# Seven block products for eight: the output product of a gated linear unit as 2x2 blocks, in a kernel whose instruction order is planned

## The chip, the cores and the metric

One core of one Trainium2 chip. The metric is the device time of one execution in microseconds (us), median of several; the profile adds the span of one profiled execution, which is some 2 us shorter. Engines are named as in the profile: PE = TensorE (matmul), PEld = TensorE's weight load (runs beside PE), DVE = VectorE, ACT = ScalarE, POOL = GpSimd, SP = SyncE (here: issues transfers). PSUM is the memory on the chip that this kernel's matmuls write to, in *banks*; SBUF holds the rest.

## The reference, cut to what matters

```python
# q, k, v: (8 batches, 8 heads, 576, 64); w_val, w_out: (512, 512); conv_w: (5, 512); all fp32
kv  = einsum('bhsd,bhse->bhde', k, v)
x   = einsum('bhsd,bhde->bhse', q, kv)
x   = x / sqrt(mean(x*x, -1) + 1e-6) * g_norm        # then heads are put side by side: (8, 576, 512)
gate_pre[:, s] = sum over j in 0..4 of conv_w[j] * x[:, s - 4 + j]   # causal, per channel
out = (sigmoid(gate_pre) * (x @ w_val)) @ w_out
```

The last product, `gv @ w_out` with `gv = gate * val`, is the *output product*. The change is about it.

## The kernel before, in the parts that matter

Tokens of two batches are cut into nine chunks of 128; the middle one belongs to both batches. For each chunk, four matmuls of 512 columns sum over 512 channels into a PSUM bank, ScalarE copies the bank to SBUF, and SyncE stores it:

```python
def out_product(i, c):
    po = ps("mm", [P, C], f"out{i}_{c}")                 # "mm": a ring of three PSUM banks
    for jt in range(NK):                                 # NK = 4, C = 512, P = 128
        nc.tensor.matmul(po[:], gv[:, jt, c * P:(c + 1) * P], wout[:, jt, :],
                         start=(jt == 0), stop=(jt == NK - 1))
    st["po", i, c] = po

def keep_out(i, c):
    ot = work.tile([P, C], FP32, tag="ot", bufs=3, name=f"ot{i}_{c}")
    nc.scalar.copy(out=ot[:], in_=st["po", i, c][:])
    st["ot", i, c] = ot
```

What VectorE does ahead of it, per batch and group of 128 channels (four such groups): four *taps* of the convolution on 576 tokens, each reading what the one before wrote, and two *gatings* that read the value product from a PSUM bank of the same ring of three:

```python
def gate_tap(b, jt, tap):
    gate = st["gate", b, jt]
    nc.vector.scalar_tensor_tensor(
        out=gate[:], in0=xTs[b % 3][:, jt, tap * TB:tap * TB + S],
        scalar=cwT[:, tap, jt:jt + 1], in1=gate[:], op0=ALU.mult, op1=ALU.add)

def gated(b, jt, n):
    first = b % 2 * S + n * SV
    nc.vector.tensor_tensor(
        out=gv[:, jt, first:first + SV], in0=st["val", b, jt, n][:],
        in1=st["gate", b, jt][:, n * SV:(n + 1) * SV], op=ALU.mult)
```

Nothing of this is issued in the order of the text. Every step is given to a planner with its engine, an assumed duration, a wished time, and what it needs, takes and frees; the planner finds one order for all engines, and the instructions are issued in it. Each engine then works through its own queue strictly in order. A table of shifts, found by search, moves the wished times:

```python
SHIFTS = {"gate_start": {0: 7}, "gate_tap": {3: 16.5, 7: 9}, ...}      # cut: 22 kinds of steps

def add(self, engine, time, want, fn, *args, needs=(), gives=(), takes=(), frees=(), ...):
    ...
    want += SHIFTS.get(fn.__name__, {}).get(which[0] if len(which) == 1 else which, 0.0)
    ...
...
    for step in plan.order():
        step["fn"](*step["args"])
```

Of the kernel before, what the change touches and what calls it, by code (L numbers as in the profile page):

```python
# [15 lines left out]
P = 128  # L16
# [5 lines left out]
    "gate_start": {0: 7},  # L22
    "gate_tap": {3: 16.5, 7: 9},
    "gated": {0: 14.5, 6: -13.5},
    "halo": {2: -0.5, 4: -69, 6: -5.5},
    "kv_product": {1: -16, 6: -3},
    "load_half": {("k", 3): -7, ("k", 4): -27, ("k", 6): -21.5, ("v", 0): -5, ("v", 1): 18, ("v", 2): -5,
        ("v", 4): -34, ("v", 6): -74},
    "load_q": {3: 2.5, 4: -1, 5: -3, 6: -5, 7: -12.5},
    "load_q_rows": {0: -273, 1: 28.5},  # L30
    "load_tails": {0: -53, 3: -20.5, 4: 24},
    "move_blocks": {3: 35, 7: 5.5},
    "narrow_weight": {("wout", 1): -14.5, ("wout", 2): -68},
    "normalise": {2: -16.5},
    "out_product": {2: -291.5},
    "powers": {7: -166.5},
    "raw_product": {0: -10.5},
    "square": {1: 0.5, 5: -17.5},
    "stage_weight": {("cw", 0): -385, ("wout", 0): -43, ("wout", 3): -18.5, ("wval", 1): -83.5,
        ("wval", 2): -40, ("wval", 3): -31.5},  # L40
    "store": {0: -1.5},
    "sums": {0: -19, 2: -73.5, 4: 6},
    "turn_q": {3: -15, 5: -59.5},
    "turn_x": {0: -9.5},
    "val_product": {0: 15, 1: 47.5, 2: 72, 3: 70.5, 4: 57, 5: 52},
# [3 lines left out]
class Planner:  # L49
# [7 lines left out]
    HOP = 0.15  # L57
    LANDING = 1.9

    def __init__(self, rings, by_batch):  # L60
        self.by_batch = by_batch
        self.rings = {name: {"size": n, "taken": [], "freed": {}} for name, n in rings.items()}
        self.steps, self.done, self.pending = [], {}, []

    def add(self, engine, time, want, fn, *args, needs=(), gives=(), takes=(), frees=(), load=0.0, ahead=40.0):
# [5 lines left out]
            gives=list(gives), takes=list(takes), frees=list(frees), load=load, ahead=ahead, at=len(self.steps)))  # L71

    def ready(self, step):

        t = step["want"] - step["ahead"]
        for key in step["needs"]:
            if key not in self.done:
                return None
            when, engine = self.done[key]
            t = max(t, when + (0.0 if engine == step["engine"] else self.HOP))  # L80
        for name, owner in step["takes"]:
            ring = self.rings[name]
            n = len(ring["taken"]) - ring["size"]
            if name in self.by_batch and len(ring["taken"]) != owner:
                return None
            if n >= 0:
# [4 lines left out]
                t = max(t, when + (0.0 if engine == step["engine"] else self.HOP))  # L91
        return t

    def order(self):
        free, transfers, left, found = {}, 0.0, list(self.steps), []
        while left:
# [20 lines left out]
            for name, owner in step["frees"]:  # L117
                self.rings[name]["freed"][owner] = end, step["engine"]
# [6 lines left out]
def kernel(  # L125
# [10 lines left out]
):  # L136

# [47 lines left out]
    def ps(kind, shape, name):  # L185
# [3 lines left out]
        "k0": 2, "k1": 2, "v0": 2, "v1": 2, "tails": 2, "q": 4, "w64": 3, "y": 2, "wexp": 2, "wman": 1,  # L189
# [20 lines left out]
    wout = const.tile([P, NK, C], FP32, name="wout")  # L210

# [77 lines left out]
    def narrow(key, dst, n):  # L289
# [40 lines left out]
        else:  # L330
            nc.vector.scalar_tensor_tensor(
                out=dst, in0=split(mf), scalar=gcol[:] if key[0] == "wval" else 2.0 ** -20, in1=split(e.bitcast(FP32)),
# [53 lines left out]
    def turn_q(b, hp):  # L386

        q, qT = st["q", b, hp], new_qT(b)[:, hp, :]
        for c in range(NJ):
            nc.vector.transpose(out=qT[:, c * P:(c + 1) * P], in_=q[:, c:NJ * HB:NJ, 0:TB])  # L390
# [109 lines left out]
    def turn_blocks(b, c):  # L500
        if ("y", b) not in st:
            st["y", b] = work.tile([P, C // TB, NJ, TB], FP32, tag="y", name=f"y{b}")
# [66 lines left out]

    def store(i, c):  # L570
# [13 lines left out]
    def before(kind, n, b):  # L584
        return [(kind, b, ORDER[n - 1])] if n else []

    def attention(b, first, step, kv_first, turn_first):

        slow = 1.7 if b == 0 else 1.0
        for hp in range(HP):  # L590
# [9 lines left out]
            if b >= TURNED:  # L600
                plan.add(
                    "DVE", 1.0, turn_first + 1.5 * hp, turn_q, b, hp,
# [4 lines left out]
            "ACT", 0.8, kv_first + 1.5 * HP, kv_copy, b,  # L607
# [3 lines left out]
        if b < TURNED:  # L611
            parts = [("qT", b, j) for j in range(NJ + 1)]
            for n, j in enumerate(ORDER):
# [9 lines left out]
                    "ACT", 0.95, turn_first + 0.8 * n + 0.8, sort_q, b, j,  # L623
# [5 lines left out]
        for n, c in enumerate(ORDER):  # L629
# [11 lines left out]
                "ACT", 0.62 * part, t + 1.0, square, b, c, needs=[("raw", b, c)], gives=[("sq", key)],  # L641
# [3 lines left out]
                "DVE", 0.7 * part, t + 1.6, sums, b, c, needs=[("sq", key)], gives=[("ss", key)],  # L645
# [7 lines left out]
                "DVE", 0.7 * part, t + 4.2, normalise, b, c, needs=[("raw", b, c), ("rt", key)],  # L653
                gives=[("x", key)], takes=[("x", key)], frees=[(bank, ("raw", key)), ("rt", key)],
            )
            if b >= TURNED and c < NJ:
                plan.add(
                    "DVE", 0.75, t + 5.5, turn_blocks, b, c,
# [9 lines left out]
                "ACT", 0.72 * part, t + 6.2, keep_x, b, c, needs=[("px", key)] + before("xT", n, b),  # L668
# [19 lines left out]
    def gates(b, first, step):  # L688
        for jt in range(NK):
            t = first + jt * step  # L690
            key = b, jt
            plan.add(
                "ACT", 0.8, t, gate_start, b, jt,
# [3 lines left out]
            for n, tap in enumerate(TAPS):  # L697
                plan.add(
                    "DVE", 0.82, t + (n + 1) * step / K, gate_tap, b, jt, tap,
# [3 lines left out]
                "ACT", 0.7, t + step, gate_end, b, jt, needs=[("gate", key, 0)],  # L703
# [3 lines left out]
    DV, DO = 2.5, 4.45  # L707
    HALVES = (range(NJ // 2 + 1), range(NJ // 2, NJ + 1))

    def products(b, first, step):  # L710
        made = []
        for jt in range(NK):
            for n in range(NV - 1, -1, -1):
# [4 lines left out]
                    needs=[("xT", b, c) for c in HALVES[n]] + [("wval", jt)],  # L718
                    gives=[("val", key)], takes=[("mm", ("val", key))],
# [3 lines left out]
                    "DVE", 0.46, t + 2.0, gated, b, jt, n,  # L723
                    needs=[("val", key), ("gate", (b, jt))] + [("gv", k) for k in made], gives=[("gv", key)],
                    takes=[("gv", b)] if jt == 0 and not last else [],
# [4 lines left out]

    def outputs(b, first):

        chunks = range(NJ + 1) if b % 2 == 0 else range(NJ + 1, 2 * NJ + 1)
        for n, c in enumerate(chunks):
            t = first + n * DO
            key = b // 2, c
            used = [b, b + 1] if c == NJ else [b]
# [126 lines left out]
```

## Time and profile before

| | before |
|---|---|
| time, median of 4 runs | 352.77 us (352.19 to 353.3) |
| profiled span | 350.3 us |
| TensorE busy | 327.5 us (93%) |
| VectorE busy | 235.6 us (67%) |
| batch 0 fully gated / batch 1's first gating | 69.9 / 77.8 us |

The two times in the last row are landmarks: the starts of the last instruction `gv<-val,gate` of batch 0, and of the first of batch 1, in VectorE's timeline. The page's second part cuts the span into 40 slices; each digit is the busy share in tenths (PEclk: the granted TensorE clock in tenths). Of the kernel before:

```profile
PE   3576998999999999999999999999999999999994
DVE  3366999899885779459957557997656088980000
PEclk9968999999999999999999999999999999999999
```

TensorE has holes only in the first seven slices, some 60 us, and at the very end. VectorE has air in most slices after the tenth. The prediction below shows the remaining lines of the kernel before.

### The profile page before, as it was taken

What the parts mean: (1) busy time and instruction counts of PE and PEld (TensorE: products, weight loads), DVE (VectorE), ACT (ScalarE), POOL (GpSimd) and SP (SyncE); (2) the same over time, 40 slices, a digit from 0 to 9 for tenths busy, and PEclk for the clock granted to TensorE, in tenths of its full rate; (3) what the DMA queues carried; (4) which work ended last, traced back from release to release, by engine and by line L of the source; (5) the groups of instructions that cost most, each with busy time, mean ns of one, the idle gap of its engine ahead of it and who ended that gap; (6) DMA issues with size and microseconds to landing.
All of it is one profiled execution on the core that took longest, in us unless ns stands there. A gap on an engine that the chain in (4) does not pass through costs nothing.

```text
span 350.3 us, 5671 instructions
## 1 busy us (share of the span) xinstructions
PE 327.5 (93%) x1969; PEld 221.6 (63%) x1969; DVE 235.6 (67%) x484; ACT 124.5 (36%) x229; POOL 128.0 (37%) x178
## 2 busy tenths in 40 slices
PE   3576998999999999999999999999999999999994
PEld 2565877887566557754787457745886467774441
DVE  3366999899885779459957557997656088980000
ACT  3745887173412251243321254333112154211211
POOL 3007215433219845420169960012669930000000
PEclk9968999999999999999999999999999999999999
DMA  6999999992244978973781769923012740002232
GB/s 208 314 304 336 315 242 275 256 278 77 61 129 125 226 251 210 288 169 93 220 224 30 192 154 239 269 71 82 10 31 50 188 125 1 2 0 52 67 89 61
DMA packets 46010, 55.32 MB, mean 158 GB/s; under 512 B 15754, under 2 KB 36254, under 8 KB 45982
## 3 DMA queue, kind: packets, MB, share of 16 engines
q1 hardware_dynamic: 42750, 48.67, 50.7%
q0 software_dynamic: 3072, 6.30, 7.7%
q8 instruction: 15, 0.25, 0.3%
q14 instruction: 13, 0.11, 0.1%
q10 hardware_dynamic: 160, 0.00, 0.0%
HBM read 39.21 MB, written 9.44 MB: 139 GB/s over the span
## 4 chain that ended last, share of the span: by engine, by line
PE 78%; DVE 8%; DMA 7%; ACT 3%; POOL 2%; issue 1%; SPq 1%; DVEq 0%; ACTq 0%; POOLq 0%
PE val L540 33%; PE out L559 30%; PE raw L442 7%; DVE gate L528 4%; PE kv L369 4%; DMA w_wval<-in_moe_w_val_dram 2%; DMA xT<-y 2%; DMA q<-in_q_dram 2%; POOL rt L470 1%; PE xTps L488 1%; PE qTps L403 1%; DVE qT L390 1%; DVE ss L464 1%; DVE x L477 1%; ACT gate L522 0%
## 5 line engine op out<-in xcount | busy, mean ns | idle before, releaser
L540 PE MATMUL val<-xT,wval 128*128 128x288 f32 x512 | 129.7, 408 | 0.0
L559 PE MATMUL out<-wout,gv 128*128 128x512 f32 x288 | 125.4, 592 | 0.0
L528 DVE SCALAR_TENSOR_TENSOR gate<-xT,cwT,gate 128x576 f32<-128x576 f32 x128 | 102.7, 815 | 25.1 <-ACT gate L522 22.9
L470 POOL TENSOR_TENSOR rt<-ss,mhalf 128x8 f32<-128x8 f32 (+1 forms) x40 | 63.8, 1604 | 134.7 <-DVE ss L464 134.4
L540 PEld LDWEIGHTS val<-xT,wval 128*128 128x128 f32 x512 | 95.4, 190 | 26.8 <-issue 1.7
L559 PEld LDWEIGHTS out<-wout,gv 128*128 128x128 f32 x288 | 54.1, 190 | 63.9 <-issue 61.9
L511 POOL DMA_DIRECT2D xT<-y x96 | 52.8, 556 | 17.0 <-DVE y L503 10.7
L567 ACT COPY ot<-out 128x512 f32<-128x512 f32 x36 | 20.9, 584 | 75.9 <-DMA out_dram<-ot 40.4
L442 PE MATMUL raw<-kvbd,qT 128*128 128x128 f32 (+1 forms) x320 | 38.9, 279 | 3.3 <-DVE x L477 2.4
L442 PEld LDWEIGHTS raw<-kvbd,qT 128*128 128x128 f32 (+1 forms) x320 | 35.2, 180 | 10.0 <-issue 3.9
L456 ACT ACTIVATE sq<-raw 128x512 f32<-128x512 f32 (+1 forms) x40 | 22.1, 552 | 53.2 <-PE raw L442 53.1
L535 ACT ACTIVATE gate<-gate 128x576 f32<-128x576 f32 x32 | 21.9, 684 | 48.7 <-DVE gate L528 48.6
L549 DVE TENSOR_TENSOR gv<-val,gate 128x288 f32<-128x288 f32 x64 | 28.3, 453 | 16.0 <-PE val L540 14.6
L464 DVE TENSOR_REDUCE ss<-sq 128x8 f32<-128x520 f32 (+1 forms) x40 | 25.3, 634 | 17.4 <-ACT sq L456 17.4
L477 DVE TENSOR_TENSOR x<-raw,rt 128x512 f32<-128x512 f32 (+1 forms) x40 | 25.2, 629 | 5.9 <-POOL rt L470 5.1
L369 PE MATMUL kv<-v,k 128*64 128x64 f32 x512 | 22.3, 238 | 5.6 <-DMA k<-in_k_dram 5.6
L522 ACT ACTIVATE gate<-xT,cwT 128x576 f32<-128x576 f32 x32 | 23.0, 768 | 11.5 <-DVE gv L549 7.1
L369 PEld LDWEIGHTS kv<-v,k 128*64 128x64 f32 x512 | 19.8, 151 | 9.6 <-issue 8.6
L390 DVE STREAM_TRANSPOSE qT<-q 128x128 f32<-128x128 f32 x96 | 20.7, 274 | 0.2 <-DMA q<-in_q_dram 0.2
L403 PE MATMUL qTps<-ident,q 128*64 128x128 f32 (+1 forms) x160 | 12.2, 317 | 5.5 <-DMA q<-in_q_dram 5.5
L503 DVE STREAM_TRANSPOSE y<-x 128x512 f32<-128x512 f32 x24 | 16.9, 706 | 0.6
L403 PEld LDWEIGHTS qTps<-ident,q 128*64 128x64 f32 (+1 forms) x160 | 10.8, 171 | 6.9 <-POOL vl L218 4.3
(56 smaller groups left out, 119.5 us busy)
## 6 DMA issues: line engine op xcount, KB each, us to landing
q<-in_q_dram SPq DMA_DIRECT2D x96, 140.0 KB, 4.1
out_dram<-ot SPq DMA_DIRECT2D x144, 64.0 KB, 1.7
v<-in_v_dram SPq DMA_DIRECT2D x16, 512.0 KB, 7.7
k<-in_k_dram SPq DMA_DIRECT2D x16, 512.0 KB, 7.2
xT<-y POOLq DMA_DIRECT2D x96, 64.0 KB, 2.8
q<-in_q_dram SPq DMA_DIRECT2D x4, 512.0 KB, 5.6
w_wval<-in_moe_w_val_dram SPq DMA_DIRECT2D x4, 512.0 KB, 8.5
w_wout<-in_moe_w_out_dram SPq DMA_DIRECT2D x4, 512.0 KB, 9.3
```

What stands on the lines that cost most here:

```text
L369: nc.tensor.matmul(kvp[r * D:(r + 1) * D, hp, :], st["k", b, half][:, h, j, :] if j < NJ else kl[:, 2 * hp + r, :], st["v", b, half][:, h, ...
L390: nc.vector.transpose(out=qT[:, c * P:(c + 1) * P], in_=q[:, c:NJ * HB:NJ, 0:TB])
L403: nc.tensor.matmul(pq[r * D:(r + 1) * D, hp, 0:m], st["q", b, half][:, h, j, :] if j < NJ else st["q", b, 2][:, 2 * hp + r, :], ident[0:m, ...
L442: nc.tensor.matmul(raw[row * m:(row + 1) * m, col * P:(col + 1) * P], st["qT", b][:, hp, c * P:c * P + m], kv_bd[b % 2][:, hp, :], start=T ...
L464: nc.vector.reduce_sum(out=ss[:, 0:n], in_=st["sq", b, c][:, 0:n], axis=AX.X)
L470: nc.gpsimd.tensor_tensor(out=rt[:, 0:n], in0=st["ss", b, c][:, 0:n], in1=mhalf[:, 0:n], op=ALU.pow)
L477: nc.vector.tensor_tensor(out=x[:, 0:n * D].rearrange("p (h e) -> p h e", h=n), in0=st["raw", b, c][:, 0:n * D].rearrange("p (h e) -> p h ...
L511: nc.gpsimd.dma_start(out=xTs[b % 3][i * TB:(i + 1) * TB, :, first:first + P], in_=y[a * TB:(a + 1) * TB, i])
L528: nc.vector.scalar_tensor_tensor(out=gate[:], in0=xTs[b % 3][:, jt, tap * TB:tap * TB + S], scalar=cwT[:, tap, jt:jt + 1], in1=gate[:], op ...
L540: nc.tensor.matmul(val[:], wval[:, kc, jt * P:(jt + 1) * P], xTs[b % 3][:, kc, HALO + n * SV:HALO + (n + 1) * SV], start=(kc == 0), stop=( ...
L549: nc.vector.tensor_tensor(out=gv[:, jt, first:first + SV], in0=st["val", b, jt, n][:], in1=st["gate", b, jt][:, n * SV:(n + 1) * SV], op=A ...
L559: nc.tensor.matmul(po[:], gv[:, jt, c * P:(c + 1) * P], wout[:, jt, :], start=(jt == 0), stop=(jt == NK - 1),)
```

## The change

Intent: two chunks of tokens (rows) by the two halves of the channels (columns of `gv`), times `w_out` in 2x2 blocks, is a 2x2 block product. Strassen's scheme, in Winograd's form, does it with seven block products instead of eight, at the price of sums on the inputs and outputs. Sixteen pairs of chunks are done so; the four middle chunks stay as they were.

- Input sums on VectorE: four `token_sums` for two pairs (512 elements each, 32 in all), and four `weight_sums` once.
- Each block product is two matmuls of 256 columns. Partial results a and c share one PSUM bank, b has its own. Two *keeps* of 256 columns per pair are copies on ScalarE, and five are additions on VectorE, in step with the products.
- To pay for it, VectorE's taps of two gates take turns, so that no tap directly follows the one that it reads; and four 128-wide transposes of q become one 512-wide.
- The planner gets shorter durations and a cost for waits within an engine, value products must be issued in their order, and the table of shifts is new: the whole order was searched again. One ring of buffers (`y`, between two transposes) shrinks from two to one.

The core of the diff, cut:

```diff
-    "gate_start": {0: 7},
-    "gate_tap": {3: 16.5, 7: 9},
+    "gate_start": {0: 29.5, 1: -9, 3: 2},
+    "gate_tap": {1: 22.5, 2: 40.5, 3: 71, 4: 84.5, 5: 61.5, 6: 70.5, 7: 83.5},
 ... (the whole table is new)
-        for c in range(NJ):
-            nc.vector.transpose(out=qT[:, c * P:(c + 1) * P], in_=q[:, c:NJ * HB:NJ, 0:TB])
+        nc.vector.transpose(
+            out=qT[:, 0:SF].rearrange("p (c a t) -> p c a t", c=NJ, a=HB),
+            in_=q[:, 0:NJ * HB, 0:TB].rearrange("p (a c) t -> p c a t", c=NJ))
 ...
+    def weight_sums(n):
+        ...
+        nc.vector.tensor_tensor(out=wsum[:, n], in0=one, in1=two, op=ALU.subtract)
+    def token_sums(i, h, n):
+        ...
+        nc.vector.tensor_tensor(out=new, in0=one, in1=two, op=op)
+    def fast_product(i, p, n):
+        ...
+        bank, tokens, weights_ = (
+            ("a", chunk(0, EVEN), wout[:, EVEN, LOW]), ("b", total(1), wsum[:, 1]),
+            ("c", total(0), wsum[:, 0]), ("b", total(2), wsum[:, 2]),
+            ("a", chunk(0, ODD), wout[:, ODD, LOW]), ("c", total(3), wout[:, ODD, HIGH]),
+            ("b", chunk(1, ODD), wsum[:, 3]))[n]
+        if n == 0:
+            both = ps("mm", [P, 2, C // 2], f"ac{i}_{p}")
+            st["a", i, p], st["c", i, p] = both[:, 0], both[:, 1]
+            st["b", i, p] = ps("mm", [P, C // 2], f"b{i}_{p}")[:]
+        for k in range(NK // 2):
+            nc.tensor.matmul(
+                st[bank, i, p], tokens()[:, k], weights_[:, k],
+                start=(n < 2 and k == 0), stop=(k == NK // 2 - 1), skip_group_check=True)
+    def fast_keep(i, p, n):
+        ... (n = 0 and 4: copies on ScalarE)
+        nc.vector.tensor_tensor(out=out_, in0=one, in1=two, op=ALU.add)
 ...
-            t = first + jt * step
+            t = first + jt // 2 * 2 * step
 ...
-                    "DVE", 0.82, t + (n + 1) * step / K, gate_tap, b, jt, tap,
+                    "DVE", 0.735, t + (n + 1) * 2 * step / K, gate_tap, b, jt, tap,
 ...
-                    needs=[("xT", b, c) for c in HALVES[n]] + [("wval", jt)],
+                    needs=[("xT", b, c) for c in HALVES[n]] + [("wval", jt)] + [("val", k) for k in made],
```

## The prediction

> **What bounds the kernel now.** I read first the busy line and the forty slices: TensorE is busy 93% of the span, and nearly all of the missing 7% lies in the first sixth. I then cut the span by hand into stretches (columns: length, then busy time and instruction count of TensorE, weight load, VectorE, ScalarE, GpSimd, then granted clock, DMA share and GB/s):
>
> ```profile
> PE 327.5 (93%) x1969; PEld 221.6 (63%) x1969; DVE 235.6 (67%) x484; ACT 124.5 (36%) x229; POOL 128.0 (37%) x178
> ...
> 0.00:58.00 58.00, 41.07 (x519) 35.14 (x520) 40.10 (x92) 37.42 (x81) 15.33 (x21) 0.91 1.01 282
> 58.00:150.00 92.00, 92.00 (x535) 63.44 (x534) 73.19 (x162) 31.25 (x56) 46.18 (x59) 1.00 0.71 196
> 150.00:180.00 30.00, 29.16 (x177) 18.14 (x176) 24.74 (x53) 10.07 (x18) 5.87 (x4) 1.00 0.64 171
> 180.00:315.00 135.00, 135.00 (x673) 91.79 (x672) 97.55 (x182) 40.46 (x67) 60.62 (x94) 1.00 0.40 100
> 315.00:351.00 36.00, 30.29 (x71) 13.11 (x69) 0.00 (x0) 5.27 (x9) 0.00 (x0) 0.99 0.25 66
> ```
>
> Two stages. Up to 58 us loads, weight conversion and the first batch's chain leave TensorE idle for 16.9 us. From 58 to 345 us it has one gap (0.84 us) and sets the end. VectorE is at 80% from 58 to 150 us, 72% from 180 to 315 us, and does nothing in the last 31 us. "Busy" is no proof of full rate, so I took rates from the chain of work that ended last, read in order of time, where each row is a run of back-to-back instructions:
>
> ```profile
> 265.29 0.89 PE raw L442 x8
> 266.18 17.17 PE out L559 x40
> 283.35 31.04 PE val L540 x128
> 314.39 27.48 PE out L559 x64
> ```
>
> **What one instruction costs.** The same rows give 17.17/40 = 429.3 ns for an output instruction (512 columns) and 31.04/128 = 242.5 ns for a value instruction (288 columns). The line through both is 0.834 ns a column plus 2.3 ns; it gives 215.8 ns for the new 256 columns. At 128 columns it gives 109 ns, and the raw product's rows show 0.89/8 = 111 ns, so the line holds below 256 too, though a weight load is recorded at 190 ns: it is hidden already at 128 columns. One written matmul is two recorded instructions. For VectorE the timeline of that engine gives start-to-start times, which is what a queue pays:
>
> ```profile
> 94.40 0.70 DVE L503 STREAM_TRANSPOSE y<-x 128x512 f32<-128x512 f32 x1
> ...
> 96.18 0.88 DVE L390 STREAM_TRANSPOSE qT<-q 128x128 f32<-128x128 f32 x4
> 96.98 0.20 DVE L391 STREAM_TRANSPOSE qT<-q 128x64 f32<-128x64 f32 x1
> 97.11 0.85 DVE L390 STREAM_TRANSPOSE qT<-q 128x128 f32<-128x128 f32 x4
> ...
> 303.30 3.25 DVE L528 SCALAR_TENSOR_TENSOR gate<-xT,cwT,gate 128x576 f32<-128x576 f32 x4
> ...
> 306.46 0.82 DVE L549 TENSOR_TENSOR gv<-val,gate 128x288 f32<-128x288 f32 x2
> ```
>
> The four taps of one gate start 0.81 us apart, each waiting for the one before; the gating that follows and does not need the last tap starts 3.16 us after the first, before that tap's end (306.55). So about 0.08 us of a tap is a tail that only a dependent instruction pays. Two gatings take 0.82 us where one is recorded at 0.46: 0.37 each, from one start to the next. Four 128x128 transposes cost 0.80 us.
>
> **What the Trainium skill says.** (1) "TensorE: Matmul & The Clock Gate", Back-to-back issue gap: N/2.4 + 2.5 ns warm, with a warning that in a stream it may be off either way. For two passes, 2N/2.4 + 2.5 gives 429.2, 242.5 and 215.8 ns: the trace agrees. (2) "FP8 and Floating Point Precision", TensorE Precision Notes: true FP32 takes four passes; two records of two passes each agree. So a saved block product is worth its full four passes. (3) "VectorE: DVE Perf Modes", the section on the TRN2 errata: every Vector instruction pays a fixed cost on top of its elements. It agrees (0.37 us for 288 elements, 0.62 for 512), which is why many 256-wide keeps are dear. (4) "PSUM — Partial Sum Buffer", bank collisions: two engines may not touch one bank at once, even in different columns. The new a and c halves share a bank, so TensorE has to wait while a or c is read; no run yet shows the cost.
>
> **The change part by part.** *TensorE.* A pair of chunks took 16 recorded instructions: 16 x 429.3 = 6.87 us. It now takes 7 block products of two matmuls, 28 instructions: 28 x 215.8 = 6.04 us. 0.83 us saved in each of 16 pairs is 13.2 us; four single chunks stay. All of TensorE's work, summed in this way over the compiled order, falls from 321.5 to 308.4 us. *ScalarE.* 32 full copies go, 32 half copies come; it is at 36% and this frees some 6 us. *VectorE.* Added: 80 keeps of 256 elements x 0.35 us (0.37 less 32 elements) = 28.0; 32 token sums x 0.61 = 19.5; four weight sums = 2.4; in all 49.9 us. Removed: four transposes become one of 512 wide, 0.80 to 0.62 us, 24 times = 4.3; and taps in turns: 61 of 128 taps followed their own gate's tap directly, now none does, 61 x 0.08 = 4.9. Net about +39: 235.6 becomes about 274 us. *Where it lies.* In the steady stage TensorE is on the path, so its 13.2 us are real as long as VectorE follows. Some 6 us of the added VectorE work falls into the last 16 us, where it was idle.
>
> **The handover from start-up.** I summed both engines' work along the compiled order up to the same landmarks. Gating of batch 0 finishes after 51.4 us of VectorE work (before 53.0); batch 1's first gating is issued after 76.9 (before 61.1), because the weight sums, the first token sums and the first keeps now stand ahead of it. VectorE had been idle for 15.9 us when its first tap began (40.8 us on the clock, 24.9 us of work), and from then to 58 us for only some 2 more. The new order puts 27.1 us of work ahead of the first tap, so I take 15.5 us of idle: batch 0 is gated at about 67 us. TensorE has then done only 42.2 us of its work (47.9 in the kernel before, at about 71 us), as its order follows VectorE's; 266.2 us are left. From there to batch 1's first gating both have equal loads, 25.5 and 25.8 us. If nothing stalls: 67 + 266 + 5 (last matmul to end, as now) = 338 us of span. From batch 1's to batch 5's last gating VectorE has 122 us of work against TensorE's 137, 89%. In-order queues at such a load will miss each other: I choose 2.5 us for 67 to 93 us, 2 for the rest and 0.7 for the last group's token sums, which follow the last gating directly. That gives a span of 343.4; runs were 1.8 to 2.9 us longer than the profiled span, so 345.7 us, 2.1% less than now.
>
> **The rivals.** *A, the whole saving arrives:* span 337, time 339 to 340. For it: the order was searched again with waits of its own, and the old order left TensorE only 0.84 us of gap. Against: the start-up stage is not TensorE's, and VectorE was busy 19.5 of the 20 us from 40 to 60 us. *B, VectorE becomes the bound:* each pair needs five keeps in step with the products, behind 0.74 us taps in a strict queue; a keep that is late by one tap stops the next product on that bank, since a product lasts only 0.86 us. One such miss of 0.5 us a pair is 8 us, and the time is 350 to 353. For it: 80 new waits of this kind. Against: over long stretches VectorE still has 11% free, and the final two pairs have it to themselves. *C, output buffers:* two of the three output tiles are now held for a whole pair until their last quarter is added, so a keep may wait for a store, with all VectorE work behind it. ScalarE's copies show waits labelled with the store in the kernel before, though each copy came as soon as its matmul was done. In back-to-back pairs I expect up to half a microsecond; with other work between them nothing. It would put the time at 347 to 350. *D, slower than now* needs over 13 us of new gaps; nothing shows that much.
>
> **Range and chances.** A is the floor, B nearly the ceiling, and my sum lies between them: 340.0 to 351.5 us. The 2% line lies at 346.1, just above my figure, so faster by over 2% gets 0.55, within 2% 0.44, slower 0.01.
>
> **What would show it.** Right: 256-column instructions at 216 ns in runs, so output work at about 110 us of TensorE; VectorE busy near 274 us with taps in turns starting about 0.74 us apart; gaps of TensorE from 60 us on of some 4 to 8 us in all, most of them before 100 us and released by VectorE; the last 16 us without gaps but one. Wrong: a block product whose instructions take clearly over 216 ns (bank or weight-load effects); a first gating of batch 1 well before or after 93 us; waits of keeps for stores above 0.5 us; or TensorE gaps spread evenly over the pairs, which would be rival B.

## The result, and the profile after

| | before | after | after, repeated (e5) |
|---|---|---|---|
| time, median | 352.77 us (352.19 to 353.3) | 348.02 us (347.49 to 348.76) | 347.25 us (346.83 to 347.8) |
| ratio to before, 95% interval | | 0.9867 (0.984 to 0.9894) | 0.9827 (0.9806 to 0.9848) |
| profiled span | 350.3 us | 346.0 us | 345.8 us |

A ratio here is always the mean time of one kernel's fast runs over that of the other's fast runs of the same rounds on the same chip, so it is not quite the ratio of the medians. The change is 1.3 to 1.7% faster: correct, real, and under the 2% line, where 345.7 us had been predicted. The page of the kernel after:

```profile
span 346.0 us, 6161 instructions
...
PE 318.6 (92%) x2161; PEld 257.2 (74%) x2161; DVE 273.2 (79%) x528; ACT 117.4 (34%) x229; POOL 131.9 (38%) x178
...
PE   0865979999999999999999999999999999999994
DVE  4619699999999689988996998999459986765520
PEclk9997699999999999999999999999999999999999
```

TensorE fell by 8.9 us of recorded busy time, though 13.1 us of its work went (worked out in the prediction). Busy time hides short waits, because the recorded ends of matmuls are modelled: between the landmarks of the account below, `--windows` has 267.1 us of busy time for 262.8 us of work in the kernel after, and 271.0 for 270.2 in the kernel before. VectorE's zeros at the end are mostly filled. Now the same stretches of both kernels (columns: length, then busy time and instruction count of PE, PEld, DVE, ACT, POOL, then granted clock, DMA share, GB/s); first before, then after:

```profile
0.00:40.00 40.00, 24.66 (x317) 21.71 (x318) 22.62 (x63) 22.60 (x48) 11.81 (x19) 0.87 1.02 299
40.00:68.00 28.00, 26.42 (x255) 21.70 (x254) 26.63 (x57) 18.43 (x40) 9.08 (x9) 1.00 1.00 262
68.00:93.00 25.00, 25.00 (x184) 17.79 (x183) 23.41 (x41) 11.98 (x21) 9.02 (x6) 1.00 0.51 152
93.00:340.00 247.00, 246.16 (x1206) 158.36 (x1205) 162.92 (x326) 70.29 (x120) 98.09 (x145) 1.00 0.49 127
```

```profile
0.00:40.00 40.00, 22.55 (x237) 19.46 (x238) 23.05 (x64) 23.57 (x49) 11.92 (x19) 0.89 0.95 265
40.00:68.00 28.00, 25.18 (x234) 19.83 (x233) 25.77 (x48) 16.39 (x35) 2.64 (x2) 0.98 0.88 252
68.00:93.00 25.00, 24.50 (x251) 20.94 (x251) 24.69 (x46) 10.74 (x21) 11.23 (x10) 1.00 0.83 235
93.00:340.00 247.00, 245.40 (x1449) 196.87 (x1444) 199.65 (x372) 66.17 (x125) 106.11 (x147) 1.00 0.49 127
```

From 93 to 340 us TensorE's recorded busy time lacks only 1.6 us (0.8 in the kernel before). The start-up looks worse: 47.7 us of TensorE busy time up to 68 us, against 51.1. Both kernels ran a part of it at a lowered granted clock (0.87 and 0.89 up to 40 us). The new instructions themselves run as planned. In PE's timeline, the start times of successive block products of one pair (four recorded instructions each):

```profile
327.37 1.03 PE L628 MATMUL b<-wsum,sums 128*128 128x256 f32 x4
328.23 1.03 PE L628 MATMUL ac<-wout,gv 128*128 128x256 f32 x4
329.10 1.03 PE L628 MATMUL ac<-wout,sums 128*128 128x256 f32 x4
329.96 1.03 PE L628 MATMUL b<-wsum,gv 128*128 128x256 f32 x4
```

The steps are 0.86 to 0.87 us, 216 ns an instruction. (The 1.03 us is from the first start to the modelled end of the last, so it holds a tail that the next product does not wait for. Read the steps, not the lengths.) And VectorE's taps, nine in a row:

```profile
44.69 6.64 DVE L545 SCALAR_TENSOR_TENSOR gate<-xT,cwT,gate 128x576 f32<-128x576 f32 x9
```

That is 0.73 us from one to the next, if the last has its recorded 0.81.

**The account of TensorE's time.** For both kernels I took TensorE's work in issue order (prediction: 321.5 and 308.4 us; 47.9 and 42.2 us of it issued before batch 0 is fully gated) and compared it with the clock at two landmarks: batch 0 fully gated, and the start of the last chunk's output product (3.43 us of work), which stands at about 341.7 us before and 337.37 us after.

| stretch | before: clock, work, lost | after: clock, work, lost | change in lost |
|---|---|---|---|
| start to batch 0 fully gated | 69.9, 47.9, 22.0 | 68.2, 42.2, 26.0 | +4.0 |
| from there to the last chunk | 271.8, 270.2, 1.6 | 269.2, 262.8, 6.4 | +4.8 |
| last chunk to end of span | 8.6 | 8.6 | 0 |

So 13.1 us of work went, 8.8 us came back as lost time, and 4.3 us are left: 350.3 less 346.0. The experiments ask what the two losses are.

The second loss can be read from PE's timeline, if one goes by start times. An example from the kernel after:

```profile
265.16 1.03 PE L628 MATMUL ac<-wsum,sums 128*128 128x256 f32 x4
266.36 1.13 PE L628 MATMUL b<-wsum,sums 128*128 128x256 f32 x4 [0.17 <-DVE ot L651]
268.02 1.13 PE L628 MATMUL ac<-wout,gv 128*128 128x256 f32 x4 [0.53 <-DVE ot L651]
```

Four instructions of 0.86 us in all start at 265.16, yet the next starts 1.20 us later: 0.33 us are lost where the page shows 0.17. Taken so for every step between the two landmarks, with 2.3 ns + 0.834 ns a column as the price, the kernel after has eight waits that cost 3.4 us (2.1 by the page), and the step behind each is another 0.1 us longer, 0.8 in all; the kernel before has one wait, 0.9 us in all. Steps into or out of the narrower matmuls (`128*64` in the form: kv and some of the raw products) are 0.1 us longer too: 38 of them, 3.8 us, against 26, 2.5 us, in the kernel before. That makes 3.3 and 1.2 of the 4.8 us. (My prices of the narrow instructions hold part of the second kind, so the changes compare here, not the levels.)

### The profile page after: what moved, and what is told of

It reads as the page before. It is cut to its first block, busy times and chain, and to the rows that moved or that the text cites. A ratio compares the mean times of both kernels' runs of the same rounds, so it can differ in the third digit from the quotient of the medians.

```text
span 346.0 us, 6161 instructions
## 1 busy us (share of the span) xinstructions
PE 318.6 (92%) x2161; PEld 257.2 (74%) x2161; DVE 273.2 (79%) x528; ACT 117.4 (34%) x229; POOL 131.9 (38%) x178
## 4 chain that ended last, share of the span: by engine, by line
PE 81%; DVE 6%; DMA 5%; ACT 4%; SPq 1%; issue 1%; DVEq 0%; ACTq 0%
PE val L557 37%; PE ac L628 15%; PE b L628 10%; PE raw L459 8%; PE kv L385 5%; PE out L576 3%; DMA w_wval<-in_moe_w_val_dram 2%; DMA q<-in_q_dram 2%; PE xTps L505 2%; PE qTps L420 2%; DMA out_dram<-ot 1%; DVE ot L651 1%; DVE ss L481 1%; SPq L657 1%; DVE x L494 1%
## 5 line engine op out<-in xcount | busy, mean ns | idle before, releaser
L557 PE MATMUL val<-xT,wval 128*128 128x288 f32 x512 | 133.2, 413 | 3.0 <-DVE gv L566 2.8
L545 DVE SCALAR_TENSOR_TENSOR gate<-xT,cwT,gate 128x576 f32<-128x576 f32 x128 | 99.0, 810 | 1.2 <-ACT gate L539 1.1
L628 PE MATMUL ac<-wout,gv 128*128 128x256 f32 x128 | 33.6, 385 | 0.8 <-DVE ot L651 0.8
L628 PE MATMUL b<-wsum,sums 128*128 128x256 f32 x128 | 33.5, 384 | 0.7 <-DVE sums L611 0.5
L628 PEld LDWEIGHTS b<-wsum,sums 128*128 128x128 f32 x128 | 23.2, 190 | 5.1 <-DVE sums L611 0.9
L628 PEld LDWEIGHTS ac<-wout,gv 128*128 128x128 f32 x128 | 23.3, 190 | 4.8 <-DVE ot L651 1.6
L644 ACT COPY ot<-ac 128x256 f32<-128x256 f32 x16 | 5.9, 371 | 47.8 <-PE ac L628 45.7
L385 PE MATMUL kv<-v,k 128*64 128x64 f32 x512 | 20.3, 225 | 1.2 <-DMA v<-in_v_dram 1.2
L385 PEld LDWEIGHTS kv<-v,k 128*64 128x64 f32 x512 | 17.7, 138 | 4.9 <-issue 4.1
L651 DVE TENSOR_TENSOR ot<-ac,ot 128x256 f32<-128x256 f32 x16 | 6.8, 425 | 13.8 <-ACT ot L644 13.8
```

Source lines behind the costliest of these rows:

```text
L385: nc.tensor.matmul(kvp[r * D:(r + 1) * D, hp, :], st["k", b, half][:, h, j, :] if j < NJ else kl[:, 2 * hp + r, :], st["v", b, half][:, h, ...
L545: nc.vector.scalar_tensor_tensor(out=gate[:], in0=xTs[b % 3][:, jt, tap * TB:tap * TB + S], scalar=cwT[:, tap, jt:jt + 1], in1=gate[:], op ...
L557: nc.tensor.matmul(val[:], wval[:, kc, jt * P:(jt + 1) * P], xTs[b % 3][:, kc, HALO + n * SV:HALO + (n + 1) * SV], start=(kc == 0), stop=( ...
L628: nc.tensor.matmul(st[bank, i, p], tokens()[:, k], weights_[:, k], start=(n < 2 and k == 0), stop=(k == NK // 2 - 1), skip_group_check=True)
```

## The experiments

Twelve kernels ran. For each I read the same landmarks:

| kernel | time, us | ratio to before | batch 0 fully gated | batch 1 first gating | last chunk starts | last chunk less batch 0 gated |
|---|---|---|---|---|---|---|
| before | 352.77 | 1 | 69.9 | 77.8 | 341.7 | 271.8 |
| after | 348.02 | 0.9867 | 68.2 | 93.4 | 337.37 | 269.2 |
| e1 thin keeps | 346.01 | 0.9808 | 68.3 | 93.4 | 335.39 | 267.1 |
| e2 thin sums | 345.83 | 0.9799 | 70.9 | 95.4 | 338.66 | 267.8 |
| e3 eight products | 359.8 | 1.0179 | 68.9 | 94.3 | 349.68 | 280.8 |
| e4 taps only | 358.25 | 1.0128 | 69.7 | 85.5 | - | - |
| e5 after again | 347.25 | 0.9827 | 68.0 | 93.2 | 337.23 | 269.2 |
| e6 x first | 346.83 | 0.9819 | 67.3 | 92.5 | 336.41 | 269.1 |
| e7 late wval | 350.98 | 0.994 | 72.5 | 97.7 | 341.65 | 269.2 |
| e9 kv first | 347.17 | 0.9824 | 67.9 | 93.1 | 337.07 | 269.2 |
| e10 kv first, VectorE | 349.21 | 0.9877 | 70.5 | 95.7 | 339.66 | 269.2 |
| e11 no shifts | 390.96 | 1.1064 | 62.9 | 78.9 | - | - |
| e12 kv in the gap | 347.46 | 0.9847 | 67.0 | 92.2 | 336.18 | 269.2 |
| e13 gap and weight sums | 346.47 | 0.9822 | 66.9 | 92.2 | 335.87 | 269.0 |

The intervals of neighbouring kernels overlap, so differences of 1 to 2 us between experiments rest on the landmarks, which repeat: the last column is 269.0 to 269.2 in eight runs. The theory that I started from: after the start-up TensorE is the bound, and VectorE's 38 us cost little. The main rival: VectorE's keeps and sums are what took back the gain.

### e1: keeps of 32 columns (wrong)

Twelve per cent of the keep's width, in the same order; the output is wrong. The output tiles became three fixed ones, cleared at the start, so that nothing unwritten is stored.

```diff
-        nc.vector.tensor_tensor(out=out_, in0=one, in1=two, op=ALU.add)
+        nc.vector.tensor_tensor(out=out_[:, 0:32], in0=one[:, 0:32], in1=two[:, 0:32], op=ALU.add)
```

> Wrong result on purpose: every keep of VectorE adds 32 columns in place of 256; the order of all engines is that of the changed kernel. VectorE loses 80 x 0.233 = 18.6 us of work. My theory (TensorE's saving of 13 us is cut by about 4 us more lost in start-up and some 3 to 4 us of small stalls later, part of them waits for keeps): 1 to 4 us faster than the changed kernel, 344 to 347 us. Rival 1, VectorE is now the bound of the steady stage: 8 us faster or more, below 340. Rival 2, start-up alone: no change, 347.5 to 348.5.

Measured: 346.01 us, ratio 0.9808 (0.9756 to 0.9859). VectorE's busy time fell by 17.3 us to 255.9, and TensorE's steady stretch got 2.1 us shorter. Counted from batch 0's last gating, 0.3 us of it comes at a wait at 143.6 us, 0.9 us at waits between 264 and 273 us, and the rest from 312 us on; keeps end most of these waits in the kernel after. So 17 us of keeps cost the end 2 us, not 17. Rival B, as a bound, is out.

### e2: sums of 16 or 32 columns (wrong)

```diff
-        nc.vector.tensor_tensor(out=wsum[:, n], in0=one, in1=two, op=ALU.subtract)
+        nc.vector.tensor_tensor(out=wsum[:, n, :, 0:32], in0=one[:, :, 0:32], in1=two[:, :, 0:32], op=ALU.subtract)
...
+        w = P if (i, h) in ((0, 0), (0, 1)) else 16
-        nc.vector.tensor_tensor(out=new, in0=one, in1=two, op=op)
+        nc.vector.tensor_tensor(out=new[:, :, :, 0:w], in0=one[:, :, :, 0:w], in1=two[:, :, :, 0:w], op=op)
```

The first two groups of token sums keep their width, the tiles of the sums became three fixed ones, and `wsum` was cleared at the start.

> Wrong result on purpose: the four weight sums and the token sums of all groups but the first two write 64 elements in place of 512, order unchanged. VectorE loses 28 x 0.467 = 13 us, 1.9 us of it (the weight sums) before batch 1's first gating. My theory: batch 1's first gating 1 to 2 us earlier than 93.4 us, and the time 1 to 3 us less than the changed kernel's 348. Rival 1, VectorE is the bound: 5 us or more. Rival 2, the start-up chain before 60 us alone: no change.

Measured: 345.83 us, ratio 0.9799 (0.9749 to 0.9849); VectorE 11.8 us less busy. The profiled run is the slowest of the four (349.08 us), with a slow start-up (batch 0 gated 2.7 us late, granted clock 0.85 from 40 to 68 us); from there on it is 1.4 us shorter: 0.7 us at 74.8 us, where TensorE no longer waits for a copy of ScalarE, and 0.7 us at 325.5 us, where it no longer waits for sums. The two thin versions together show that at most some 3.5 of the 4.8 us lost in the steady stretch are VectorE's; they were not run together, so this sum is an upper estimate, not a measurement. It fits the account by start times, where the waits that VectorE ends cost 3.5 us.

### e3: the last block product issued twice (wrong)

```diff
-        for k in range(NK // 2):
-            nc.tensor.matmul(
+        for again in range(2 if n == 6 else 1):
+            for k in range(NK // 2):
+                nc.tensor.matmul(
```

> Wrong result on purpose: the last block product of each pair is issued twice, so TensorE has eight products again with every other instruction and wait of the change. TensorE gains 16 x 0.863 = 13.8 us of work. My theory: TensorE is the bound after 60 us with some 4 us of slack in all, so 10 to 13 us slower than the changed kernel, 358 to 361 us. If VectorE is the bound: less than 6 us slower, below 354. If every microsecond of TensorE is on the path: 361.8.

Measured: 359.8 us, ratio 1.0179 (1.0145 to 1.0213); 64 instructions more, 64 x 215.8 ns = 13.8 us of TensorE's work, and the steady stretch grew by 11.6 us. So a block product in the steady stage is on the path with 84% of its length: this is what a saved product is worth. The other 2.2 us fill waits that the kernel after has: by start times, three waits are left of the eight, 2.0 us in place of 4.2. TensorE is the bound there. With eight products the new order, with its sums and keeps, takes 7 us more than the kernel before.

### e4: taps in turns and the wide transpose alone

The kernel before with these two parts of the change, the order of value products as after, and the old planner and table of shifts. The result is correct.

> The kernel before with only the two changes that unload VectorE: taps of two gates in turns and one transpose for four. Output product as before, the order planned anew with the old shifts. VectorE loses 9 us. My theory: in the steady stage this is worth nothing; in start-up the chain of taps shortens by up to 2 us: 350.5 to 353 us, same. Rival: these two and not the seven products brought the gain: about 348.

Measured: 358.25 us, ratio 1.0128 (1.0097 to 1.0159): 1.3% *slower* than before, a clear miss. VectorE's busy time fell by 6.5 us (235.6 to 229.1), but TensorE got a hole of 3.7 us at 86 us, waiting for a gating, and batch 1 was fully gated at 116.0 us instead of 108.8. The steps carry less work and yet end later, because the old table was searched for other steps. The experiment does not price the taps; it says that a half-applied change with an order searched for something else measures the order. What the taps in turns are worth in time stays open.

### e5: the changed kernel again

No edit: a repeat, to see how far the start-up repeats from run to run and chip to chip.

> The changed kernel itself, as the base of this call's comparisons. 347.5 to 349, ratio to before 0.987 within 0.003. Its profile shows whether start-up (last gating of batch 0, 68.2 us in the first profile) repeats to within 1 us.

Measured: 347.25 us, ratio 0.9827. The stretch of lowered clock falls elsewhere (1.0 up to 20 us in both, then 0.83 and 0.91 in the next two stretches of 20 us, where the first run had 0.77 and 0.97), but batch 0 is fully gated within 0.2 us of the first run, and the steady stretch is 269.2 us in both. Inside the start-up the runs differ more: batch 0's first gating starts at 50.3 us, 52.1 in the first run.

### e6, e7: moving single steps of the start-up

e6 puts one value product (2 us of TensorE) behind the last transpose of x, for which the first taps wait. e7 loads and converts one quarter of `w_val` after the first q, k and v.

```diff
+        move(("turn_x", 0, 0), "val_product", 0, 0, 1)                                  # e6
```
```diff
+        move(("load_half", "v", v, 0, 1), "stage_weight", "wval", 3)                    # e7
+        for n in range(8):
+            move(("sort_q", 0, 0) if n == 0 else ("narrow_weight", "wval", 3, n - 1), "narrow_weight", "wval", 3, n)
```

> One instruction group moved: batch 0's first value product stands behind the transposes of its last chunk, not ahead of them, on TensorE alone. In the changed kernel this product ran at the lower clock (3.8 us from 37.4 us) and the transposes behind it held back the first gates of the batch until 43.3 us. My theory (the missing part of the gain is lost by TensorE in the first 60 us, after which it is the bound): first tap near 41.5 us, last gating of batch 0 at about 66.5, time 1 to 2 us less. Rival, VectorE's added work before batch 1's first gating sets the pace: that gating stays at 93.4 us and the time does not change (within 0.5 us).

> The weight block that is needed last (fourth quarter of the value weights) is loaded after the first keys and values and converted after the first, not ahead of the queries. Queries, keys and values then arrive 0.5 MB earlier, 1.6 us at 330 GB/s. My theory: TensorE's first transposes start 1.5 us earlier (8 in place of 9.6 us) and the time falls by 0.5 to 1.5 us, as part of it is caught by later waits in start-up. Rival as before: no change.

Measured: e6 346.83 us (0.9819), 0.8 us earlier than e5 at the gating of batch 0 and at every landmark after it. On the ratio that is no difference that the intervals would carry. e7 350.98 us (0.994), 3.7 us slower, a miss with the wrong sign. The reason is a queue. In ScalarE's timeline of e7, the copy of the kv blocks, which TensorE's first raw products need, stands behind a weight conversion that now waits for a later load:

```profile
26.21 0.72 ACT L325 ACTIVATE wexp_wval<-wexp_wval,biases 128x512 uint32<-128x512 uint32 x1 [2.95 <-DVE wexp_wval L320]
26.84 0.73 ACT L395 COPY kvbd<-kv 64x256 f32<-64x256 f32 x2
```

TensorE's first transposes of q did start earlier, at 7.1 us (9.6 in the kernel after). (The 330 GB/s of the expectation lies near the fastest start-up slices of the pages: 336 GB/s before, 352 after.) That gain was eaten by a step that had nothing to do with q. But both kernels teach the same thing through the last column of the table: wherever the start-up ends, the rest takes 269.1 to 269.2 us.

### e8: refused

> Both moves together, and the copy of batch 0's key-value product ahead of one weight conversion on ScalarE. My theory: 2 to 3.5 us less than the changed kernel, 344.5 to 346. Rival: no change.

It moved the kv copy ahead of the matmuls whose result it reads (a read of PSUM that nothing has written). It never ran; e9 and e10 make the point that it was meant for.

### e9, e10: mending what e7 showed

```diff
+        move(("turn_x", 0, 0), "val_product", 0, 0, 1)                                  # e9 and e10
+        move(("kv_copy", 0), "narrow_weight", "wval", 1, 1)
+        move(("sums", 0, 4), "narrow_weight", "wval", 1, 4)                             # e10 only
+        for n in range(5, 8):
+            move(("normalise", 0, 4) if n == 5 else ("narrow_weight", "wval", 1, n - 1), "narrow_weight", "wval", 1, n)
```

> The order of e6, and one more move on ScalarE: the copy of the first batch's kv blocks (kvbd) goes ahead of a weight conversion step that waits for a late weight load. In e6 the copy began 0.6 us after that step at 22.3 us, though its matmuls had ended at 21.3. Theory (the start-up's offset is carried through to the end one to one, TensorE being the bound after it): the first raw product begins 1.0 to 1.3 us earlier, batch 0 is gated 0.5 to 1.3 us earlier (67.3 in e6, 68.2 in the changed kernel) and the time falls by the same, to about 0.5 to 1.5 us under the changed kernel. Rival (VectorE's load after the start-up, or waits of the steady stage, set the end): a move in the start-up alone gives nothing beyond the 0.3 us of e6. A third outcome, seen in e6 and e7: the gain is swallowed within the start-up by another wait; then batch 0's gating does not come earlier, and nothing is learnt about the rest.

> As e9, and on VectorE the last four steps of one weight conversion (0.4 to 0.7 us each, for a weight that is not needed before 46 us) go behind the first chunk's sum and normalising, which had stood behind them. Theory: the first normalised chunk, ready at 28.4 us in e6, comes 1.5 to 2.5 us earlier, the first transposes of x with it; the later chunks are paced by their own sums, so batch 0 is gated 0.5 to 1.5 us before e9 at most, and the time follows one to one. Rival: the first chunk's delay is hidden anyway, since later chunks set the first tap: no change from e9 (within 0.3 us).

Measured: e9 347.17 us (0.9824), e10 349.21 us (0.9877). In e9 the raw products start at 21.94 us (e6: 23.10) after a wait of 0.83 instead of 1.84 us, as meant. The 1.2 us did not arrive (batch 0 is gated 0.6 us later than in e6), because the next step waits on VectorE:

```profile
21.94 3.53 PE L459 MATMUL raw<-kvbd,qT 128*64 128x128 f32 x32 [0.83 <-ACT kvbd L395]
28.30 0.44 PE L505 MATMUL xTps<-ident,x 128*128 128x128 f32 x2 [2.83 <-DVE x L494]
```

The normalised x came at the same time as before, since its queue held weight conversions ahead of it. e10 takes those away: the first x comes 0.7 us earlier, but the weight steps now stand ahead of the later chunks' sums, the second x comes 1.3 us later than in e9, and batch 0 is gated 2.5 us later. This was the third outcome of my expectation: the gain was swallowed inside the start-up. What e9 and e10 add is two more start-up ends (67.9 and 70.5 us) with the same 269.2 us after them.

### e11: the planned order without its searched shifts

```diff
-        want += SHIFTS.get(fn.__name__, {}).get(which[0] if len(which) == 1 else which, 0.0)
```

> The changed kernel with the table of searched shifts emptied: the same instructions, in the order that the planner finds from its wishes alone. It measures how much of the time is the order. e4, where half of the change ran with a table searched for another kernel, lost some 4 to 5 us in waits. Theory (order carries a large part): 5 to 15 us slower than the changed kernel, with most of it in the start-up and at batch 1's gating, where queues of loads, weights and taps compete. Rival (the instructions' sum alone sets the time, the order is a detail): within 2 us of the changed kernel. Instruction times and busy times should be as before within 1 us for TensorE and VectorE in either case.

Measured: 390.96 us, ratio 1.1064 (1.1018 to 1.1111), 12.6% over the changed kernel, with the same instructions (VectorE's busy time 275.3 us, against 273.2). I had expected 5 to 15 us, and most of it in the start-up. It was 43 us, and the start-up was *better*: batch 0 is gated at 62.9 us. The loss comes later, as waits of TensorE of every kind (columns: in all, times, longest, us):

```profile
PE raw L458 <- DVE x L493: 14.0, 3, 9.5
PE val L556 <- DVE gv L565: 11.3, 4, 4.0
PE ac L627 <- DVE ot L650: 6.3, 6, 1.8
PE qTps L419 <- DMA q<-in_q_dram: 5.0, 3, 4.1
PE kv L384 <- DMA v<-in_v_dram: 4.9, 2, 3.0
```

That is near to rival B of the prediction: with the same instructions in another order, normalised x, gatings and keeps that come too late stop TensorE, though VectorE is busy for only 71% of the span. Not all of the 43 us is waiting: TensorE's own busy time is 11.1 us longer (329.7 against 318.6), at a granted clock of 0.94 over the span where the changed kernel has 0.98 (0.83 from 80 to 100 us, 0.89 from 120 to 180, where that kernel has 1.00). The waits and the lower clock come together in this run; it does not separate them. In the changed kernel the same waits sum up to little:

```profile
PE qTps L420 <- DMA q<-in_q_dram: 3.7, 3, 3.2
PE val L557 <- DVE gv L566: 2.8, 1, 2.8
...
PE ac L628 <- DVE ot L651: 0.8, 2, 0.5
...
PE b L628 <- DVE sums L611: 0.5, 1, 0.5
```

### e12, e13: filling TensorE's new gap, and taking the weight sums off VectorE

The 2.8 us wait in the second line is at 49.8 to 52.6 us: the fourth value product needs the bank of the first, whose gating needs the first gate; and as the taps of two gates take turns now, that gate ends only with its neighbour's. The kernel before gates its first product no earlier (52.7 us), but TensorE has raw and kv matmuls to do meanwhile, up to 53.8 us. e12 puts batch 1's kv matmuls (2.4 us) there, and loads their k ahead of batch 2's, which had gone first. e13 also computes the four weight sums on GpSimd.

```diff
+        ... (the loads of k of batches 1 and 2 change places)                           # e12 and e13
+        ... (kv_product(1, 0..3) go ahead of val_product(0, 1, 0))
-        nc.vector.tensor_tensor(out=wsum[:, n], in0=one, in1=two, op=ALU.subtract)      # e13 only
+        nc.gpsimd.tensor_tensor(out=wsum[:, n], in0=one, in1=two, op=ALU.subtract)
```

> The changed kernel with two moves. TensorE has one gap of 2.82 us at 49.8 to 52.6 us, where the fourth value product waits for a PSUM bank whose gating waits for both gates of the first pair. The kv matmuls of batch 1 (2.4 us), which stand behind that product, go ahead of it, and so that they can run there the loads of k of batch 1 change places with those of k of batch 2, which were issued 12 us before them. The gap should shrink to about 0.4 us, and TensorE will have done 44.6 instead of 42.2 us of its work when batch 0 is gated (68.2 us). Theory (TensorE's loss in the start-up is carried to the end): the time falls by 2 us, if VectorE lets it. Rival (from batch 0's last gating to batch 1's first, 25.2 us with VectorE busy 99%, VectorE is the bound, as the order was planned so that both have equal loads): batch 1's first gating stays within 0.5 us of 93.4 us, TensorE gets new gaps of about 2 us before it, and the time falls by under 0.7 us.

> As e12, and the four weight sums (2.4 us on VectorE, all between 58 and 93 us) are computed on GpSimd in the same places of the order. Theory with TensorE alone as the bound: as e12 within 0.5 us. Rival with VectorE as the bound up to batch 1's first gating: that gating comes 1.5 to 2.4 us earlier than in e12 and the time falls by as much, to about 345 to 346 us. If GpSimd's sums take over 3 us each or come too late for the first block products, a wait for them shows on TensorE before 93 us and the gain is lost.

Measured: e12 347.46 us (0.9847), e13 346.47 us (0.9822). In e12 the gap shrank from 2.82 to 0.33 us, and a new one of 1.93 us opened six microseconds later, behind the copy of batch 1's kv blocks, which stands in ScalarE's queue where it stood:

```profile
51.69 4.15 PE L557 MATMUL val<-xT,wval 128*128 128x288 f32 x16 [0.33 <-DVE gv L566]
57.77 1.75 PE L459 MATMUL raw<-kvbd,qT 128*64 128x128 f32 x16 [1.93 <-ACT kvbd L395]
```

My expectation also had an error of its own: the kv matmuls stood ahead of batch 0's last gating already, so moving them could not raise the work done by that landmark; it could only bring the landmark nearer. From the first to the last gating of batch 0 it now takes 15.8 us (16.0 in the kernel after): 0.2 us, not 2, and less than that kernel's own two runs differ (17.7 in e5). The first gating was 0.9 us earlier too, but in e5, without an edit, it was 1.8 us earlier.

e13 tells apart what bounds the stretch from batch 0's last gating to batch 1's first, where VectorE is busy 24.69 of 25 us. On VectorE the stretch lost 2.4 us:

```profile
68.00:93.00 25.00, 24.54 (x271) 20.72 (x268) 22.30 (x41) 11.09 (x22) 15.52 (x15) 1.00 0.81 227
```

and batch 1's first gating came at 92.2 us, as in e12: 25.3 us after batch 0's last, where e12 and the kernel after take 25.2. So the 99% on VectorE did not set this landmark in e13; TensorE was busy for 98%. VectorE is not quite free there, though: e2, which makes the weight sums thin on VectorE itself, has 24.5 us for the same stretch, 0.7 us less. Why e13 shows nothing of this is open; the moves of e12, which it shares, brought waits of their own.

No version that computes the right result beat the changed kernel beyond the intervals: e5, e6, e9, e12 and e13 lie between 0.9819 and 0.9847, each interval some 0.004 to 0.007 wide.

## Why the prediction was right or wrong, point by point

- **216 ns for a 256-column instruction, 0.83 us a pair, 13.1 to 13.2 us of TensorE's work: right.** Steps of 0.86 to 0.87 us for four; e3 shows the price on the path, 84% of a product's length.
- **VectorE near 274 us: right (273.2), with luck.** The prediction's own terms make 49.9 - 9.2 = 40.7 us, not 39, so 276.3 us. e4 removed 6.5 us of busy time, not 4.3 + 4.9 = 9.2; the added keeps and sums are then 273.2 - 229.1 = 44.1 us, not 49.9. The errors cancel in part.
- **Taps in turns some 0.74 us apart: right (0.73).** Their worth in time was not shown: e4 measured the order with them.
- **Batch 0 gated at about 67 us: 68.2, 68.0 in the repeat.** The first term that was too small, by 1.2 us, is VectorE's idle time before this landmark. The prediction put the first tap at 27.1 + 15.5 = 42.6 us and let no idle time follow, though the kernel before has some 2 us of it there. The first tap began at 43.3 us, and 0.9 us of idle time followed; in e5 it began at 42.1 us, and 1.6 us followed, most of it waits of gatings for value products. So a late first tap is not the whole cause. In the first run it waits for the gate that ScalarE starts, which waits for the last transpose of x, behind a value product that took 3.84 us by start times at a lowered clock, against 1.94. e6, without it in the way, has the first tap and the landmark 0.8 us before e5.
- **Both engines equally loaded to batch 1's first gating at about 93 us: right (93.4), with luck.** With the 2.5 us of stalls that the sum has for this stretch, it would have been 95.3. The stretch took 25.2 us on the clock, without them, but began 1.2 us late.
- **4 to 8 us of gaps from 60 us on, most of them before 100 us and released by VectorE: wrong in place.** The visible gaps sum to 2.1 us: 0.51 (ScalarE) at 74.8 us, then 0.17 and 0.53 us at 266 to 268 us (VectorE's keeps), 0.48 at 325.5 (token sums; I had said 0.7), 0.23 at 334.7, and three of 0.1 us or less. By start times these eight waits cost 4.2 us, 0.7 of it before 100 us; VectorE ends all but the first, as predicted. The losses sum to 6.4 us from 68 us on, where my stalls were 5.2. This is the second term that was too small, by 1.2 us. What the stalls left out are steps into and out of narrow matmuls, 0.1 us each: the kernel before has them too, but the new order has 38 of them behind the landmark, not 26. e1 and e2 give 2.1 and 1.4 us of the 6.4 to VectorE's load.
- **The sum: 343.4 us of span predicted, 346.0 measured: +1.2 for the start-up, +1.2 for the losses after it, 0.2 for the last stretch and rounding.** The mechanism held: a real saving of 13 us cut down by a start-up whose order gives TensorE less to do, and by small misses after it. The time lay in the range, but the class that I held likelier (over 2% faster, 0.55) was missed: 1.3% and 1.7%. The figure lay on the line: 2% below the 352.77 us of these runs is 345.7, too.
- **Rival A (all arrives)** fell: 4.3 of 13.1 us arrived. **Rival B (VectorE the bound)** fell for this order (e1, e3); in another order late steps of VectorE stop TensorE (e11). **Rival C (output buffers)** shows twice: 0.19 us at 157.7 us, and 0.96 us in the last pair, twice the half microsecond that I had expected and above what I had named as a sign of being wrong. In VectorE's and PE's timeline of the kernel after:

```profile
334.19 0.42 DVE L651 TENSOR_TENSOR ot<-ac,u 128x256 f32<-128x256 f32 x1 [0.96 <-DMA out_dram<-ot]
...
334.67 1.13 PE L628 MATMUL ac<-wout,gv 128*128 128x256 f32 x4 [0.23 <-DVE ot L651]
```

  A keep waits 0.96 us for a store to free its tile, and TensorE loses 0.23 us by it (0.4 by start times), so the rival stays small.

**What was shown and what was not.** Shown: TensorE is the bound after the start-up (e3 against e1); where the start-up ends is carried to the end one to one (eight runs from 66.9 to 72.5 us, each followed by 269.0 to 269.2 us); the order is worth more than the change (e11). Not shown: how to end the start-up earlier without loss later. Six edits by hand moved single steps; they gained 1.1 us at most at that landmark against e5, and in e7, e9, e10 and e12 another queue took over. That TensorE has 5.7 us less of its work behind it at that landmark is the account's reading of the searched order; no experiment changed this amount alone, and whether another order avoids it, no run here tells. Nor was the kernel before run with its own order searched again, so a part of the gain may be the new search and not the seven products.

## What to carry to other kernels

A saving on the bounding engine has to be followed to a landmark: ask how much of that engine's work is already behind it when the steady stage begins, because an order that feeds another engine first gives part of the saving back there, and here everything after that was a fixed offset. A second engine at 99% in some stretch need not be the bound; take work off it, and see whether the next landmark moves, before you try to relieve it. And in strictly ordered queues an experiment that adds, removes or halves steps also changes the order: here the order alone was worth 43 us, and the change 5 to 6.

## What the Trainium skill lacked or had wrong

- "TensorE: Matmul & The Clock Gate", Back-to-back issue gap: the warm formula, taken for two passes, holds in this kernel's streams to 0.1 ns at 512 and 288 columns (429.3 and 242.5 ns), and the 256-column products step by 216 ns; its warning that a stream may be off either way was not needed here. No page has a figure for a change of shape (it would belong to "TensorEngine Tiling (Array Packing)"): here each step into or out of the `128*64` matmuls is 0.1 us longer, so that value products that follow them take 2.14 us for eight instructions, against 1.94 us elsewhere.
- The same page, What's actually happening, gives two clock states, full and half. The slices of these profiles show means of 0.6 and 0.7 in the start-up, which fits a switching between two states; the traces here do not resolve it. It says that the place of the switch varies from run to run, and that agrees: 0.77 and 0.97 for 20 to 40 and 40 to 60 us in one run, 0.83 and 0.91 in the next, with the landmarks equal to 0.2 us.
- "VectorE: DVE Perf Modes", The DRAIN you can't avoid, says that the next operation starts when the pipe of the one before is empty, and that one which is not held starts earlier. Its one measurement, of eight copies with and without semaphores, has no difference. Here the taps that read what the one before wrote start 0.81 us apart, and taps in turns 0.73 us: a dependence costs 0.08 us.
- "PSUM — Partial Sum Buffer", bank collisions: it warns, which no run here tests, but there is no figure for what it costs to keep two halves of one bank apart by waits. In this kernel it is small: the page has 0.8 us in all of waits of products on the shared bank for keeps (1.1 us by start times).
- No page has a figure for what decided this case: with the same instructions in strictly ordered queues, the order itself was worth 43 us of 348 (e11), lowered clock included.
